# The first tile of a two-layer MLP begun by halves of 256 tokens, with attention of the second half between

## The chip, the cores and the metric

The kernel runs on one core of one Trainium2 chip. The metric is device time in microseconds (us). Engines are TensorE (PE, with its weight loads shown apart as PEld), VectorE (DVE), ScalarE (ACT), GpSimd (POOL) and SyncE (SP); SP, ACT and POOL issue DMAs, and 16 DMA engines carry them. Each engine works through its instructions in the order in which they were written.

## The reference

Local attention with 8 memory rows, then two MLPs whose hidden activations differ.

```python
for c in range(nc):                                   # chunks of 32 queries
    l_start, r_end = max(0, c*32 - 16), min(S, c*32 + 32 + 8)
    k_full = concat([mem_k, k[:, :, l_start:r_end]], axis=2)
    v_full = concat([mem_v, v[:, :, l_start:r_end]], axis=2)
    scores = scale * (q_c @ k_full.T)
    a = exp(scores - max(scores)); a = a / (sum(a) + 1e-9)
    out[:, :, chunk] = a @ v_full
x = out as (3072 tokens, 512)
h = x @ w_in;   g = maximum(0.01 * h, h);   y = g @ w_out          # 512 -> 2048 -> 512
h = y @ w_in2;  g = P(h) / (Q(h) + 1e-6);   out = g @ w_out2       # P, Q polynomials
```

There are 4 batches, 8 heads of 64, 768 positions. w_in, w_out and the second layer's weights come as 64-bit floats.

## The kernel before

The 3072 tokens are cut into 6 tiles of 512 (NMAX), a tile into 4 blocks of 128. Attention works on blocks, numbered j from 0. The hidden width of 2048 is cut into 16 pairs f: the 128 columns of w_in and the 128 rows of w_out that belong together. One pair on one tile is an h (`emit_h`, 12 matmuls into a bank "hps": 4 steps over 512 inputs, 3 products each) and a y (`emit_y`, 12 matmuls into the four banks "acc", which gather over all pairs). Each fp32 number is carried as a high and a low part: xh and xl for the activations, wih/wil and woh/wol for the weights, gh and gl for the hidden values, and the three products are high x high, high x low and low x high. Between h and y, ACT makes gh and s (`leaky`), and DVE makes gl from them.

Weights arrive as raw 64-bit words (tile "wr", three buffers, 512 KB a load) and pass four steps: `load_w` issues the DMA on SP, `scale_w` is an ACT instruction (ww from wr), `join_w` three DVE instructions (ww), `split_w` an ACT cast (wih or woh) and a DVE subtraction (wil or wol). `weights0` does one of each for the first layer: cast of one half-pair, scaling of the one two further on, join of the next, subtraction, and a further load. The list `halves` sets the order of the half-pairs, "i" for w_in and "o" for w_out.

Attention of a block is a row of functions: `mid_load_q`, `mid_load_k`, `mid_load_v` issue its DMAs; `mid_a` transposes q and k on PE (psq, psk) and copies them on ACT (qT, pb); `mid_s` makes the scores on PE (pss) and on DVE their maxima and differences (mx, t); `mid_e` is the exponential on ACT; `mid_n` the division on DVE (sm, t); `mid_p` transposes the weights on PE (pst) with a copy on ACT (pm); `mid_x` the weighted sums on PE (psx), then xh by ACT and xl by DVE. Blocks 0 to 3, the whole first tile, come in a prologue that is written out line by line; blocks 4 to 7 go between the matmuls of the first tile, and later ones are made by another route between those of later tiles.

Nothing reorders: the written order is each engine's order. After the prologue a loop goes over `items`, one for each layer, tile and pair; `advance_h` runs h two items ahead of y, and in the first tile calls `weights0` for each h from the third on, while another `weights0` follows each y. k and v of blocks 0, 1 and 2 stand in three different buffers (`room`): kb and vb, and the still unused tiles xh and xl of the second token tile.

Of the kernel before, what the change touches and what calls it, by code (L numbers as in the profile page):

```python
# [9 lines left out]
F32 = mybir.dt.float32  # L10
# [6 lines left out]
P = 128  # L17
LCTX, RCTX, CHUNK = 16, 8, 32
NEG = -1.0e30
WIDE_FROM = 2  # L20


@with_exitstack
def kernel(
# [76 lines left out]

    halves = []
    for layer in range(2):
        for f in range(FC + 2):
            if f < FC:
                halves.append((layer, "i", f))
            if f >= 2:
                halves.append((layer, "o", f - 2))

# [116 lines left out]
    LAST = WIDE_FROM * FIRST  # L226
    spare = [xpool.tile([P, 2, 2 * H * D], F32R, tag=t, name=t).bitcast(F32) for t in ("xh", "xl")]
    room = [(kw, vflat), (spare[0][:, 0], spare[0][:, 1]), (spare[1][:, 0], spare[1][:, 1])]
    mem_in = {}
    mq, mqT, mm = {}, {}, {}  # L230

    def home(j):
        return j if j < len(room) else 0

# [16 lines left out]
    def mid_load_k(j):  # L251
        bi, blk = divmod(j, WPS)
        t = room[home(j)][0].rearrange("p (n h d) -> p n h d", n=2, h=H)
        eng = nc.gpsimd if j else nc.sync
        if mem_rows("k", j, bi):
            for n in range(2):
                for row in (0, NM + CTX):
                    eng.dma_start(out=t[row:row + NM, n], in_=mem_k[bi].rearrange("h p d -> p h d"))
# [368 lines left out]
    def emit_y(c):  # L627
        layer, i, f = items[c]
        s0, n = tiles_of[layer][i]
        if f == 0:  # L630
            acc[i] = [psa.tile([P, 512], F32, tag="acc", name="acc") for _ in range(KC)]
        gh, gl = gt.pop(c)
        wh, wl = wt[0, "o", f]
        for d in range(KC):
            ws = slice(d * P, (d + 1) * P)
            for m, (w_, g_) in enumerate(((wh, gh), (wh, gl), (wl, gh))):
                nc.tensor.matmul(acc[i][d][:, :n], w_[:, ws], g_,  # L637
                                 start=(f == 0 and m == 0), stop=(f == FC - 1 and m == 2))
        if f == FC - 1:
# [46 lines left out]
    with tc.manual_schedule():  # L686
        nc.scalar.preload_act_table_set("natural_log_exp_and_others")
        make_identity(nc, ident)
        nc.vector.memset(kb[0][0:32], 0.0)
        for hh in range(2):  # L690
            nc.vector.memset(vw[hh * WIN:hh * WIN + 32, 0], 0.0)
        nc.vector.memset(lnb, ONE * 2.0 ** -LN_SHIFT)
        nc.vector.memset(expb, -LN_SHIFT * math.log(2.0))
        mid_load_q(0)
        mid_load_k(0)
        mid_load_v(0)
        load_w(FC * 2)
        for j in (1, 2):
            mid_load_q(j)
            mid_load_k(j)  # L700
            mid_load_v(j)
            if j == 1:
                load_w(FC * 2)
        mid_load_q(3)
        mid_a(0)
        mid_load_k(3)
        mid_s(0)
        mid_e(0)
        scale_w(FC * 2)
        mid_a(1)  # L710
        mid_n(0)
        mid_s(1)
        mid_p(0)
        mid_e(1)
        mid_x(0)
        mid_load_v(3)
        load_w(FC * 2)
        join_w(FC * 2)
        scale_w(FC * 2)
        mid_a(2)  # L720
        mid_n(1)
        mid_s(2)
        mid_p(1)
        mid_e(2)
        mid_x(1)
        load_w(FC * 2)
        weights0()
        mid_a(3)
        mid_n(2)
        mid_load_q(FIRST)  # L730
        mid_load_k(FIRST)
        mid_s(3)
        mid_p(2)
        mid_e(3)
        mid_x(2)
        weights0()
        mid_n(3)
        mid_p(3)
        mid_x(3)
        mid_load_v(FIRST)  # L740
        weights0()
        weights0()
        nc.sync.dma_start(out=coef[:, 0:4], in_=a.partition_broadcast(P))
        nc.sync.dma_start(out=coef[:, 4:6], in_=b.partition_broadcast(P))
# [21 lines left out]
        advance_h(LA)
        weights0()
        for c in range(len(items)):
            layer, i, f = items[c]
# [77 lines left out]
```

## Time and profile before

| | before |
|---|---|
| median of 3 runs | 1170.08 us (1169.69 to 1170.71) |
| profiled execution, its own time | 1169.41 us |
| its span | 1167.6 us |
| PE busy | 1131.2 us, 97% |
| weight loads (PEld) | 928.6 us, 80% |
| DVE busy | 771.6 us, 66% |
| ACT busy | 624.9 us, 54% |
| POOL busy | 247.5 us, 21% |
| mean granted clock of PE | 0.989 |

The span runs from the first instruction to the last; about 2 us of the execution lie outside it. A share of busy time is a mean over stages: the first 57 us, without wide matmuls, are hardly seen in PE's 97%. A row of the timeline gives start and length in us, engine and line, what was written from what, the shape, the count, and in brackets the idle time before it and what ended it.

### The profile page before, as it was taken

Reading aid. Unit: us, or ns where it says so; the run is one execution under the profiler, and the core shown is the slowest. Engines: PE = TensorE matmul, PEld = TensorE weight load, DVE = VectorE, ACT = ScalarE, POOL = GpSimd, SP = SyncE. Lnnn points to the kernel's source line nnn. Section 1 sums busy time; section 2 is a strip of 40 time slices with the busy share of each in tenths; the row PEclk is TensorE's granted clock in tenths of the full one; section 3 lists DMA queues with packets and bytes.
Section 4 is the critical chain, followed back from the end, with each engine's and each line's share of the span. In section 5 each row is a group of like instructions: output and inputs, shape, how many; then the busy total and the mean of one; then the engine's idle time right before and its main releaser. Section 6 shows DMA issues by size and latency. Waiting matters only on the chain.

```text
span 1167.6 us, 20228 instructions
## 1 busy us (share of the span) xinstructions
PE 1131.2 (97%) x7808; PEld 928.6 (80%) x7808; DVE 771.6 (66%) x1361; ACT 624.9 (54%) x1135; POOL 247.5 (21%) x298
## 2 busy tenths in 40 slices
PE   5599999999999999999999999999999999999998
PEld 3487778888888888888888888888888888888887
DVE  3478865555546554554234888788788788788775
ACT  3367643223223223222344877777777777777765
POOL 6000131233211231111000222222222222222222
PEclk9699999999999999999999999999999999999999
DMA  8556788788878677852343200200200200200000
GB/s 161 136 162 197 196 226 231 198 219 243 212 202 228 197 214 223 228 170 70 131 131 91 90 1 1 72 1 1 72 1 1 73 1 1 73 1 1 37 1 36
DMA packets 149005, 132.18 MB, mean 113 GB/s; under 512 B 63473, under 2 KB 119377, under 8 KB 148909
## 3 DMA queue, kind: packets, MB, share of 16 engines
q1 hardware_dynamic: 140869, 122.54, 36.5%
q0 software_dynamic: 6272, 7.92, 3.1%
q8 instruction: 62, 1.02, 0.4%
q10 hardware_dynamic: 1768, 0.43, 0.2%
q14 instruction: 34, 0.28, 0.1%
HBM read 93.06 MB, written 37.75 MB: 112 GB/s over the span
## 4 chain that ended last, share of the span: by engine, by line
PE 91%; DMA 3%; ACT 2%; DVE 2%; issue 1%; SPq 1%; ACTq 0%; DVEq 0%
PE hps L579 44%; PE acc L675 22%; PE acc L637 20%; PE psx L379 2%; DMA wr<-in_moe_w_in_dram 1%; PE pss L475 1%; ACT t L343 1%; DMA xl<-in_k_dram 1%; DVE ww L149 1%; DMA xh<-in_v_dram 0%; DMA vb<-in_v_dram 0%; SPq L262 0%; ACT ww L132 0%; DVE wol L167 0%; PE pst L364 0%
## 5 line engine op out<-in xcount | busy, mean ns | idle before, releaser
L615 POOL TENSOR_TENSOR gl<-R,gh 128x512 fp32r<-128x512 f32 x96 | 125.7, 1309 | 502.1 <-ACT gh L614 459.9
L589 ACT ACTIVATE gh<-hps 128x512 fp32r<-128x512 f32 x96 | 57.5, 599 | 291.6 <-PE hps L579 291.6
L592 DVE TENSOR_TENSOR gl<-s,gh 128x512 fp32r<-128x512 f32 x96 | 66.3, 691 | 191.6 <-ACT s L590 188.4
L579 PE MATMUL hps<-xh,wih 128*128 128x512 f32 x384 | 154.0, 401 | 2.3 <-ACT pm L365 1.9
L637 PE MATMUL acc<-gh,woh 128*128 128x512 f32 x384 | 150.8, 393 | 0.0
L579 PE MATMUL hps<-xl,wih 128*128 128x512 f32 x384 | 150.8, 393 | 0.0
L579 PE MATMUL hps<-xh,wil 128*128 128x512 f32 x384 | 150.7, 392 | 0.0
L637 PE MATMUL acc<-gl,woh 128*128 128x512 f32 x384 | 149.6, 389 | 0.0
L637 PE MATMUL acc<-gh,wol 128*128 128x512 f32 x384 | 149.5, 389 | 0.0
L579 PE MATMUL hps<-yh,wih 128*128 128x512 f32 x384 | 149.4, 389 | 0.0
L579 PE MATMUL hps<-yl,wih 128*128 128x512 f32 x384 | 149.4, 389 | 0.0
L579 PE MATMUL hps<-yh,wil 128*128 128x512 f32 x384 | 149.4, 389 | 0.0
L675 PE MATMUL acc<-woh,gh 128*128 128x512 f32 x384 | 149.4, 389 | 0.0
L675 PE MATMUL acc<-wol,gh 128*128 128x512 f32 x384 | 149.4, 389 | 0.0
L675 PE MATMUL acc<-woh,gl 128*128 128x512 f32 x384 | 149.4, 389 | 0.0
L440 POOL DMA_DIRECT2D vb<-in_v_dram x128 | 83.4, 653 | 252.4 <-PE psx L379 199.6
L602 ACT ACTIVATE A<-hps 128x512 f32<-128x512 f32 x96 | 57.1, 595 | 114.0 <-PE hps L579 114.0
L618 DVE SCALAR_TENSOR_TENSOR A<-A,small,pb 128x512 f32<-128x512 f32 x96 | 72.0, 750 | 56.5 <-ACT pb L603 56.5
L579 PEld LDWEIGHTS hps<-xh,wih 128*128 128x128 f32 x384 | 72.7, 189 | 18.8 <-ACT pm L365 2.3
L609 DVE SCALAR_TENSOR_TENSOR A<-A,pb 128x512 f32<-128x512 f32 x96 | 66.5, 692 | 30.0 <-ACT pb L622 30.0
L579 PEld LDWEIGHTS hps<-xh,wil 128*128 128x128 f32 x384 | 72.8, 190 | 15.4
L579 PEld LDWEIGHTS hps<-xl,wih 128*128 128x128 f32 x384 | 72.8, 190 | 14.6 <-DVE xl L388 0.2
(107 smaller groups left out, 2017.4 us busy)
## 6 DMA issues: line engine op xcount, KB each, us to landing
wr<-in_moe_w_in_dram SPq DMA_DIRECT2D x32, 512.0 KB
wr<-in_moe_w_out_dram SPq DMA_DIRECT2D x32, 512.0 KB
park_dram<-pb SPq DMA_DIRECT2D x16, 512.0 KB
pb<-park_dram SPq DMA_DIRECT2D x64, 128.0 KB
w_dram<-ww SPq DMA_DIRECT2D x32, 256.0 KB
wb<-w_dram SPq DMA_DIRECT2D x32, 256.0 KB
kb<-in_k_dram SPq DMA_DIRECT2D x59, 112.0 KB
vb<-in_v_dram POOLq DMA_DIRECT2D x118, 56.0 KB, 3.5
```

Of the source, the lines that this page charges most:

```text
L149: nc.vector.scalar_tensor_tensor(out=wu, in0=lo32, scalar=29, in1=wu, op0=ALU.logical_shift_right, op1=ALU.bitwise_or)
L379: nc.tensor.matmul(ps[hh][e * 64:e * 64 + 64, i, c * CHUNK:(c + 1) * CHUNK], vt[r, c, 2 * i + e, :], weight(r, c, i, e), start=True, stop= ...
L440: nc.gpsimd.dma_start(out=vw[r + at:r + at + n, c], in_=v[bi, hs, lo:lo + n, :].rearrange("h p d -> p h d"))
L579: nc.tensor.matmul(ps[:, :n], w_[:, ws], x_[:, kk, :], start=(kk == 0 and m == 0), stop=(kk == KC - 1 and m == 2))
L589: nc.scalar.activation(out=gh, in_=ps, func=AF.Prelu, alpha=0.01)
L592: return [lambda: nc.vector.tensor_tensor(out=gl, in0=s, in1=gh.bitcast(F32), op=ALU.subtract)]
L602: nc.scalar.activation(out=A, in_=ps, func=AF.Square)
L609: nc.vector.scalar_tensor_tensor(out=A0, in0=A0, scalar=ONE, in1=U0, op0=ALU.add, op1=ALU.mult)
L615: nc.gpsimd.tensor_tensor(out=gl, in0=R0, in1=gh.bitcast(F32), op=ALU.subtract)
L618: nc.vector.scalar_tensor_tensor(out=A, in0=A, scalar=babs[:, 1:2], in1=U, op0=ALU.mult, op1=ALU.add)
L637: nc.tensor.matmul(acc[i][d][:, :n], w_[:, ws], g_, start=(f == 0 and m == 0), stop=(f == FC - 1 and m == 2))
L675: nc.tensor.matmul(acc[i][s], g_[:, ss], w_, start=(f == 0 and m == 0), stop=(f == FC - 1 and m == 2))
```

## The change

The 512 tokens of the first tile are taken in two halves of 256 for the first four pairs (AHEAD). The prologue does attention of blocks 0 and 1, then h and y of pairs 0 to 3 on 256 tokens, and puts blocks 2 and 3 between them. Then the same four pairs follow on the other 256 tokens, and pairs 4 to 15 on all 512. `halves` is reordered, so that the weights of pairs 0 to 3 come first. The scores and weighted sums of blocks 2 and 3 now use the PSUM banks "ps" that h uses, since "acc" is taken. k and v of blocks 0 to 3 share two buffers in turn. The memory rows of k of block 0 are issued on POOL and no longer on SP, q and k of block 0 ahead of the identity matrix.

```diff
+AHEAD = 4
...
+    HALF = NMAX // 2
+    halves = [(0, "i", 0), (0, "i", 1), (0, "i", 2), (0, "o", 0), (0, "i", 3), (0, "o", 1)]
+    for f in range(2, AHEAD):
+        halves.append((0, "o", f))
+    for f in range(AHEAD, FC + 2):
+        if f < FC:
+            halves.append((0, "i", f))
+        if f >= AHEAD + 2:
+            halves.append((0, "o", f - 2))
...
     def home(j):
-        return j if j < len(room) else 0
+        return j % 2 if j < FIRST else 0
...
     def mid_bank(j, name):
-        if j < FIRST:
+        if j < HALF // P:
             return psa.tile([P, 512], F32, tag="acc", name=name)
...
+    items = [(0, 0, f, lo, HALF) for lo in (0, HALF) for f in range(AHEAD)]
+    items += [(l, i, f, 0, tiles_of[l][i][1]) for l in range(2) for i in range(len(tiles_of[l])) for f in range(FC)
+              if (l, i) != (0, 0) or f >= AHEAD]
...
-                nc.tensor.matmul(ps[:, :n], w_[:, ws], x_[:, kk, :],
+                nc.tensor.matmul(ps[:, :n], w_[:, ws], x_[:, kk, lo:lo + n],
...
+        mid_a(0)
+        mid_load_q(2)
+        mid_load_k(2)
+        mid_s(0)
+        mid_e(0)
+        mid_a(1)
+        scale_w(FC * 2)
+        mid_n(0)
+        mid_load_q(3)
+        mid_load_k(3)
+        join_w(FC * 2)
+        mid_s(1)
+        mid_p(0)
+        mid_e(1)
+        mid_n(1)
+        mid_x(0)
+        mid_load_v(2)
+        scale_w(FC * 2)
+        weights0()
+        mid_p(1)
+        mid_x(1)
+        mid_load_v(3)
+        weights0()
+        advance_h(2)
+        weights0()
+        weights0()
+        advance_h(3)
+        emit_y(0)
+        mid_a(2)
+        mid_s(2)
+        mid_e(2)
+        weights0()
+        advance_h(4)
+        mid_n(2)
+        weights0()
+        emit_y(1)
+        mid_p(2)
+        mid_a(3)
...
+        mid_x(2)
+        mid_s(3)
+        mid_e(3)
+        weights0()
+        emit_y(2)
+        mid_n(3)
+        weights0()
+        mid_p(3)
+        emit_y(3)
+        mid_x(3)
```

What this does to the engines' order is seen at three places. On ACT, at the end of block 1's weighted sum (xh from psx; block 3's before): what stands ahead of the first hidden values gh and s, and between them. ww from wr is the scaling of newly landed weights. Before:

```order
L365 COPY pm<-pst 128x512
L387 CAST xh<-psx 128x2x128 x2
L164 CAST wih<-ww 128x512
L132 ACTIVATE ww<-wr 128x512
L164 CAST woh<-ww 128x512
L132 ACTIVATE ww<-wr 128x512
L589 ACTIVATE gh<-hps 128x512
L590 ACTIVATE s<-hps 128x512
```

Now:

```order
L373 COPY pm<-pst 128x512
L395 CAST xh<-psx 128x2x128 x2
L173 CAST wih<-ww 128x512
L141 ACTIVATE ww<-wr 128x512
L597 ACTIVATE gh<-hps 128x256
L598 ACTIVATE s<-hps 128x256
L597 ACTIVATE gh<-hps 128x256
L598 ACTIVATE s<-hps 128x256
L173 CAST wih<-ww 128x512
L141 ACTIVATE ww<-wr 128x512
```

The first gh stands two blocks earlier and behind the scaling of the fourth half-pair (it was the sixth before).

On PE, where the first matmuls of layer 1 stand, behind the weighted sum of a block (psx). Before, behind block 3:

```order
L320 MATMUL pss<-pb,qT 32x64 x32
L364 MATMUL pst<-ident,t 128x128 x4
L379 MATMUL psx<-pm,xl 64x32 x32
L364 MATMUL pst<-ident,t 128x128 x4
L379 MATMUL psx<-pm,vb 64x32 x32
L579 MATMUL hps<-xh,wih 128x512
L579 MATMUL hps<-xl,wih 128x512
L579 MATMUL hps<-xh,wil 128x512
```

Now, the middle of the first half: the end of y of pair 1, block 2's p, block 3's a, block 2's x, block 3's s, and the start of y of pair 2:

```order
L645 MATMUL acc<-gl,woh 128x256
L645 MATMUL acc<-gh,wol 128x256
L372 MATMUL pst<-ident,t 128x128 x4
L305 MATMUL psq<-ident,q_244 128x128 x4
L314 MATMUL psk<-ident,xh 128x104 x8
L387 MATMUL psx<-pm,vb 64x32 x32
L328 MATMUL pss<-pb,qT 32x64 x32
L645 MATMUL acc<-gh,woh 128x256
L645 MATMUL acc<-gl,woh 128x256
L645 MATMUL acc<-gh,wol 128x256
```

Attention of blocks 2 and 3, which stood ahead of every wide matmul, stands between the narrow ones.

On DVE, the same stretch. Before, the end of the prologue: block 2's low part, one half-pair joined and split, block 3's division and low part.

```order
L388 TENSOR_TENSOR xl<-psx,xh 128x2x128 x2
L146 TENSOR_SCALAR ww<-ww 128x512
L149 SCALAR_TENSOR_TENSOR ww<-wr,ww 128x512
L153 SCALAR_TENSOR_TENSOR ww<-wr,ww 128x512
L167 TENSOR_TENSOR wil<-ww,wih 128x512
L352 TENSOR_REDUCE sm<-t 128x8
L355 TENSOR_SCALAR sm<-sm 128x8
L356 RECIPROCAL sm<-sm 128x8
L357 TENSOR_TENSOR t<-t,sm 128x512
L388 TENSOR_TENSOR xl<-psx,xh 128x2x128 x2
```

Now, from the low part of pair 3's input weights on: gl of pair 3, block 2's division, a half-pair joined and split, block 2's low part, and the first of block 3's maxima.

```order
L176 TENSOR_TENSOR wil<-ww,wih 128x512
L600 TENSOR_TENSOR gl<-s,gh 128x256
L360 TENSOR_REDUCE sm<-t 128x8
L363 TENSOR_SCALAR sm<-sm 128x8
L364 RECIPROCAL sm<-sm 128x8
L365 TENSOR_TENSOR t<-t,sm 128x512
L155 TENSOR_SCALAR ww<-ww 128x512
L158 SCALAR_TENSOR_TENSOR ww<-wr,ww 128x512
L162 SCALAR_TENSOR_TENSOR ww<-wr,ww 128x512
L176 TENSOR_TENSOR wol<-ww,woh 128x512
L396 TENSOR_TENSOR xl<-psx,xh 128x2x128 x2
L337 TENSOR_REDUCE mx<-pss 128x4
```

A block's division stands behind a gl, which needs an h, which needs the low part of its weights; before, there was no gl in the prologue.

## Rows read from the trace of the kernel before

**Rows 1.** Waits of PE from 57 us on: total, times, longest

```profile
PE pst L364 <- DVE t L357: 2.8, 1, 2.8
PE hps L579 <- ACT pm L365: 1.9, 2, 1.0
```

**Rows 2.** Stretches: PE, PEld, DVE, ACT, POOL busy; clock; DMA share; GB/s

```profile
0.00:20.00 20.00, 8.86 (x153) 6.18 (x153) 4.77 (x15) 5.46 (x9) 15.55 (x33) 1.00 0.82 153
20.00:32.00 12.00, 8.82 (x162) 6.79 (x162) 7.33 (x17) 5.02 (x10) 2.76 (x6) 1.00 0.88 182
32.00:36.00 4.00, 4.00 (x74) 3.74 (x70) 1.89 (x5) 1.31 (x4) 0.00 (x0) 1.00 0.48 91
36.00:40.00 4.00, 0.04 (x1) 0.00 (x0) 2.84 (x6) 0.00 (x0) 0.00 (x0) 0.91 0.79 228
40.00:44.00 4.00, 1.93 (x66) 1.54 (x67) 0.40 (x1) 1.95 (x4) 0.00 (x0) 0.50 1.08 300
44.00:57.00 13.00, 5.89 (x136) 4.85 (x134) 5.93 (x14) 3.76 (x9) 0.00 (x0) 0.50 0.24 61
```

**Rows 3.** Timeline of PE in the prologue, and the first wide matmuls

```profile
27.09 0.93 PE L306 MATMUL psk<-ident,xl 104*128 104x104 f32 x4 [0.93 <-DMA xl<-in_k_dram]
...
31.66 2.03 PE L379 MATMUL psx<-pm,xh 64*64 64x32 f32 x64 [0.73 <-ACT pm L365]
33.62 1.11 PE L297 MATMUL psq<-ident,q 128*128 128x128 f32 x4
34.53 1.51 PE L306 MATMUL psk<-ident,kb 104*128 104x104 f32 x8
42.07 1.62 PE L320 MATMUL pss<-pb,qT 64*32 64x64 f32 x64 [6.02 <-ACT pb L307]
...
57.10 0.80 PE L579 MATMUL hps<-xh,wih 128*128 128x512 f32 x1 [0.36 <-ACT xh L387]
...
59.00 0.63 PE L579 MATMUL hps<-xl,wih 128*128 128x512 f32 x1
59.43 0.63 PE L579 MATMUL hps<-xh,wil 128*128 128x512 f32 x1
```

**Rows 4.** Timeline of PE behind the rise of its clock

```profile
63.22 0.39 PE L579 MATMUL hps<-xh,wil 128*128 128x512 f32 x1
...
70.98 0.60 PE L297 MATMUL psq<-ident,qr 128*128 128x128 f32 x4
```

**Rows 5.** The chain, one group of 12 wide matmuls: start, length

```profile
157.84 2.72 PE hps L579 x12
```

**Rows 6.** Timeline of ACT in the prologue

```profile
31.51 0.63 ACT L338 ACTIVATE t<-t 128x512 f32<-128x512 f32 x1
33.63 0.65 ACT L387 CAST xh<-psx 128x256 fp32r<-128x256 f32 x2 [1.49 <-PE psx L379]
...
40.47 0.66 ACT L132 ACTIVATE ww<-wr 128x512 f32<-128x512 f32 x1 [5.67 <-DMA wr<-in_moe_w_in_dram]
```

**Rows 7.** Timeline of SP's queue: the memory rows of block 0

```profile
1.42 4.21 SPq L258 DMA_DIRECT2D kb<-in_mem_k_dram  x4
```

**Rows 8.** The page's costliest groups: a weight load's row

```profile
L579 PEld LDWEIGHTS hps<-xh,wih 128*128 128x128 f32 x384 | 72.7, 189 | 18.8 <-ACT pm L365 2.3
```

**Rows 9.** Timeline of DVE in the prologue

```profile
29.79 0.42 DVE L329 TENSOR_REDUCE mx<-pss 128x4 f32<-128x256 f32 x1 [1.34 <-PE pss L320]
...
34.04 0.76 DVE L388 TENSOR_TENSOR xl<-psx,xh 128x256 fp32r<-128x256 f32 x2 [2.58 <-ACT xh L387]
34.71 0.42 DVE L146 TENSOR_SCALAR ww<-ww 128x512 uint32<-128x512 uint32 x1
...
37.10 0.68 DVE L352 TENSOR_REDUCE sm<-t 128x8 f32<-128x512 f32 x1
...
38.26 0.69 DVE L357 TENSOR_TENSOR t<-t,sm 128x512 f32<-128x512 f32 x1
```

More of the change, by code (lines that the diff above doesn't have):

```diff
@@ L95 @@
     ONE = 1.0 + 1e-6
[L102 to L108, printed above, removed]
+    HALF = NMAX // 2
[7 more added lines that the diff above has]
+            halves.append((0, "o", f - 2))
+    for f in range(FC + 2):
+        if f < FC:
+            halves.append((1, "i", f))
+        if f >= 2:
+            halves.append((1, "o", f - 2))
+    assert len(set(halves)) == len(halves) == 4 * FC
     wt, wraw, wsum = {}, {}, {}
@@ L257, in mid_load_k @@
                 for row in (0, NM + CTX):
-                    eng.dma_start(out=t[row:row + NM, n], in_=mem_k[bi].rearrange("h p d -> p h d"))
+                    nc.gpsimd.dma_start(out=t[row:row + NM, n], in_=mem_k[bi].rearrange("h p d -> p h d"))
         for n in range(2):
@@ L627, in emit_y @@
     def emit_y(c):
-        layer, i, f = items[c]
-        s0, n = tiles_of[layer][i]
-        if f == 0:
+        layer, i, f, lo, n = items[c]
+        s0 = tiles_of[layer][i][0]
+        if f == 0 and lo == 0:
             acc[i] = [psa.tile([P, 512], F32, tag="acc", name="acc") for _ in range(KC)]
@@ L636, in emit_y @@
             for m, (w_, g_) in enumerate(((wh, gh), (wh, gl), (wl, gh))):
-                nc.tensor.matmul(acc[i][d][:, :n], w_[:, ws], g_,
-                                 start=(f == 0 and m == 0), stop=(f == FC - 1 and m == 2))
+                nc.tensor.matmul(acc[i][d][:, lo:lo + n], w_[:, ws], g_,
+                                 start=(f == 0 and lo == 0 and m == 0), stop=(f == FC - 1 and m == 2))
         if f == FC - 1:
@@ L691 @@
             nc.vector.memset(vw[hh * WIN:hh * WIN + 32, 0], 0.0)
+        mid_load_q(0)
+        mid_load_k(0)
+        make_identity(nc, ident)
         nc.vector.memset(lnb, ONE * 2.0 ** -LN_SHIFT)
         nc.vector.memset(expb, -LN_SHIFT * math.log(2.0))
-        mid_load_q(0)
-        mid_load_k(0)
         mid_load_v(0)
+        mid_load_q(1)
+        mid_load_k(1)
         load_w(FC * 2)
[L698 to L716, printed above, removed]
-        load_w(FC * 2)
[L718 to L725, printed above, removed]
-        load_w(FC * 2)
[L727 to L744, printed above, removed]
+        mid_load_v(1)
+        load_w(FC * 2)
+        load_w(FC * 2)
         issued_h = [0]
@@ L751, in advance_h @@
                 emit_h(c)
-                if c < NA:
+                if items[c][0] == 0:
                     steps = leaky(c)
-                    if LA <= c < FC:
+                    if AHEAD <= c and items[c][1] == 0:
                         weights0(steps)
@@ L763, in advance_h @@
                     rational(c + 1, False, True)
+        mid_a(0)
[36 more added lines that the diff above has]
+        mid_a(3)
+        mid_load_q(FIRST)
+        mid_load_k(FIRST)
+        mid_x(2)
[8 more added lines that the diff above has]
+        mid_x(3)
+        mid_load_v(FIRST)
+        nc.sync.dma_start(out=coef[:, 0:4], in_=a.partition_broadcast(P))
+        nc.sync.dma_start(out=coef[:, 4:6], in_=b.partition_broadcast(P))
         plan()
[L766 to L769, printed above, removed]
+        advance_h(AHEAD + LA)
+        for c in range(AHEAD, len(items)):
+            layer, i, f = items[c][:3]
+            g = c - AHEAD
             if layer == 0:
-                if c == FC:
+                if g == FC:
                     nc.scalar.mul(out=ncf, in_=coef[:, 0:4], mul=-1.0)
@@ L804 @@
                 advance_h(c + 1 + look)
-            wide(2 * c + 1)
+            wide(2 * g + 1)
             if i == 0 and layer == 0:
-                weights0()
+                if f >= AHEAD:
+                    weights0()
                 if n_split[0] == FC * 2 and n_load[0] < FC * 2 + 2:
```

27 lines of the change are left out of this document (11 added, 16 removed).

## The prediction

> **What bounds the kernel now.** I read the waits of TensorE (PE) first. From 57 us to the end PE waits 2.8 us for one VectorE (DVE) instruction and 1.9 us for ScalarE (ACT) [rows 1]: from the first wide matmul on, PE is the bound, and the end moves only with the moment at which that stream begins and with what is in it. So I read next what comes before it. The stretches [rows 2] show a prologue limited by transfers and by chains across engines: the DMA engines are busy 0.82 to 0.88 of the time to 32 us, PE works 0.04 us between 36 and 40 and 5.9 of the 13 us from 44 to 57. The timeline of PE [rows 3] has the first wide matmul at 57.10 us. Those 57 us are what the change can win from.
>
> PE's speed in that prologue is the second thing to see. The granted clock reads 1.00 until 36 and 0.50 from 40 to 57 [rows 2], but four transposes of 128 columns take 1.11 us at 33.62 [rows 3] and 0.60 at 70.98 [rows 4], so I price the prologue at the lower level (1.2 GHz) from its start. The 512-column matmuls stand 0.43 us apart there (59.00 to 59.43) and 2.72/12 = 0.227 later [rows 3, 5]. The clock rose near 63.2, after PE had worked without a pause since 57.10 [rows 3, 4].
>
> **What is moved.** I call T the moment from which PE runs without stops: 57.1 before, the start of the second half's first matmul after. The stream behind T loses the first halves of four pairs: 8 groups of 12 matmuls, 96 x 0.227/2 = 10.9 us at the upper level. The same 96 stand before T instead, with two blocks of attention between them. Everything hangs on what T becomes. The change is a gain while T stays under 57.1 + 10.9 plus small terms, about 69 us.
>
> **T, first part: to the end of y of pair 0.** Before T eight halves of weights must now be cast, joined and split, not two. I count them W0 to W8 in their new order: in 0, in 1, in 2, out 0, in 3, out 1, out 2, out 3, in 4.
> - ACT stands in order, and scaling W3 now stands ahead of gh of the first two groups. In the old order ACT sat 5.67 us behind such a scaling whose weights had not landed [rows 6].
> - When W3 lands: ahead of it on the queues are q and k of four blocks, v of three (128x8x64 and 56x4x64 floats: some 3.8 MB), 0.25 MB of memory rows, and W0 to W3 of 0.52 MB each: 6.1 MB. The stretches give 20 x 153 GB/s = 3.06 MB by 20 us, 5.24 by 32, 5.61 by 36, 6.52 by 40 [rows 2], so 38 us at the old pace. Without the slack at 32 to 36 (DMA share 0.48), and with the share of wide packets that gave 300 GB/s at 40 to 44, some 32. I take 35. The four k rows of memory that leave SP's queue (4.21 us of issuing [rows 7]) start block 0 about 4 us earlier; on POOL they stand ahead of the memory rows of block 1, which so gains little.
> - The weighted sum of block 1 ended at 33.69 [rows 3]; with block 2 no longer ahead of it I take 29 to 31. Two groups behind it end at 34.5 to 36.5, about when W3 is scaled, so an earlier W3 alone would win little.
> - A 256-column matmul does not occur in the trace. At the lower level it lies between 0.23 (a 128-column transpose, 33.62 to 34.53 for four) and 0.43 (512 columns) [rows 3]; at the upper, by the same ratio of levels, between 0.12 and 0.227. I take the lower ends, since the columns alone make half of 0.43 and of 0.227. Second half at 0.12 instead of 0.113: 96 x 0.007 = +0.6 us. If the weight load showed through (0.189 each [rows 8]): 96 x 0.076 = +7.3, the upper bound.
> - From W3: scale 0.65, gh and s of two groups 4 x 0.33 [rows 6], gl 0.38, join and split together 2.39 [rows 9]: the low part of in 2 at 39.7. Its group waits for it at its third matmul; ten are left, 2.3 us: 42.0. y of pair 0: 12 x 0.23, to 44.8.
>
> The Trainium skill, "TensorE: Matmul & The Clock Gate", section on LDWEIGHTS, says that a load's time goes by its columns alone; 128 columns at 1.2 GHz are by that an estimated 107 ns. By that price the second half's loads lie just under its 0.113 of streaming and cost nothing. The row, 0.189, speaks against that and gives the upper bound; no row here has 256 columns.
>
> **T, second part: 44.8 us to the second half.** PE, ACT and DVE each keep the written order, so this is one chain. PE's order is a2, s2, h3, y1, p2, a3, x2, s3, y2, p3, y3, x3 (a transposes, s scores, p transposes of weights, x weighted sums); each group of 12 waits at its third matmul for the low part that DVE subtracts.
> 1. a2 and s2 to the first reduction: transposes 0.91 + 0.75, then 27.09 to 29.79 = 2.70 [rows 3, 9]: 4.36. DVE to the exponential: 29.79 to 31.51 = 1.72 [rows 6, 9].
> 2. join W5 and split W4, 34.71 to 37.10 = 2.39; rest of h3 2.30; gh, s, gl 0.65 + 0.38; n2 1.85 (37.10 to 38.95), which stands behind gl on DVE; join W6, split W5 2.39 [rows 6, 9]; rest of y1 2.30. To here 18.3.
> 3. p2 0.91, a3 2.42, x2 2.03, s3 1.62 on PE [rows 3]: 7.0. DVE has only x2's low part meanwhile.
> 4. scores 1.72, join and split 2.39, n3 1.85, join and split 2.39: 8.35 of DVE, over which y2 and p3 are hidden. Rest of y3 2.30, x3 2.03, cast 0.4: 13.1.
> Together 38.4, so T = 83.2. DVE's own work in it is about 19 us: half of the stretch DVE waits for PE, and half PE for DVE.
>
> **The sum.** T +26.1; moved work -10.9; narrow matmuls +0.6. The slow start of the stream, 14 matmuls in 6.12 us (57.10 to 63.22) instead of 3.2, which cost 2.9 us, is mostly over by T, as y3 and x3 run up to it without a pause: -1.9 (between 0 and -2.9). PE's waits after T: behind it DVE has per pair 2 x 2.39 and a gl, about 5.5 us, against 5.44 of PE plus attention, as before, and the lead in halves is the same by the code; I leave the 4.7 us where they are (bounds: all gone, or as much again). Sum +13.9 on the profiled execution's 1169.41 (span 1167.6): 1183.3. The median shown is 0.7 above that execution, less than a measurement can tell; I give 1183.
>
> **A rule weighed.** Between 44 and 57 us PE worked 5.9 of 13 us, with waits between, and stayed at the lower level (granted 0.50 [rows 2]). The new stretch is of that kind: matmuls for 2.3 us, then 1 to 4 us of waiting. The Trainium skill, "TensorE: Matmul & The Clock Gate", section "HAM oscillation — how this bites in real kernels", has bursts that are shorter than the waits between them fall back to the lower clock each time. The trace agrees; by that rule the time is my 1183, without it the first rival's.
>
> **The rivals.**
> - The clock rises early. PE has more to do than before (some 24 of 38 us), and h0 and h1 run without a pause. At the upper level PE's parts halve: 1.5 in a2 and s2, 3.3 in the rests of three groups, 3.5 in step 3, 1.0 in x3, 2.4 in the first part: 11.7 less, T = 71.5, +14.4 - 10.9 - 2.9 + 0.6 = +1.2: 1170.6. Against it: at 20 to 32 us PE was busy 8.8 of 12 us [rows 2] and its rows stayed long.
> - Faster: the clock rises, and W3 to W7 also land 5 us earlier, as they would if the queue held the 300 GB/s of 40 to 44 us [rows 2] from 25 us on; ACT then never stands. T = 66.5, +9.4 - 10.9 - 2.9 + 0.6 = -3.8: 1165.6. It decides at T = 69. Against it: the small packets of v lie between the weights, and the two groups behind block 1 bound it at 34.5.
> - Slower still: the weight load shows through in the second half: 1183.3 + 7.3 = 1191.
> - The change does not do what it says: if nothing of the first half overlapped the attention of the second, T would be 57.1 plus 8 x 12 x 0.23 = 22.1, so 79.2, and the time 1169.4 + 22.1 - 10.9 - 1.9 + 0.6 = 1179.3. It lies inside my range; PE's waits would tell it from the chain.
>
> **How the numbers follow.** The chain at the lower level, with W3 at 32 to 38 and single terms 2 us off, the last rival within it: 0.64, 1176 to 1189. Clock up for part or all: 0.16, 1169 to 1176. Faster rival 0.10. Slower still 0.10. The range 1170 to 1190 leaves out the faster rival, a little of the second case and half of the last. A measurement here tells 0.2% (2.3 us) from no change: faster, under 1167.7, 0.11 (the faster rival and 0.01 of the second case); within, 0.09 of the second case; slower 0.80.
>
> **What would show it.** In the new trace: ACT waits for W3 ahead of gh with PE idle around 35 us; PE waits for wil and wol before the third matmul of h2, h3, y1, y3; DVE waits for PE while p2, a3, x2, s3 run; 256-column matmuls 0.21 to 0.23 apart before T and 0.11 to 0.12 behind; T at 80 to 85. I am wrong if T lies under 70, if the first half's rows show 0.12 spacing, or if PE waits over 9 us behind T.

## The result, and the profile after

The changed kernel takes 1177.95 us (median of 4 runs, 1177.03 to 1180.84) against 1170.39 us for the kernel before beside it (4 runs, 1169.69 to 1171.24): ratio 1.0068, 95% interval 1.0050 to 1.0087. It is slower, by 7.6 us; 1183 was predicted, some 13 us slower, within 1170 to 1190. The profiled execution of the changed kernel is its slowest, 1180.84 us with a span of 1179.1.

T, the moment from which TensorE (PE) runs without stops, is 80.38 us, against 57.10 before [rows 3]; 80 to 85 was expected. The timeline of PE, changed kernel: the end of block 1's sum, four places in the first half, the start of the second half.

```profile
29.01 2.30 PE L387 MATMUL psx<-pm,xh 64*64 64x32 f32 x64 [0.73 <-ACT pm L373]
31.65 0.58 PE L587 MATMUL hps<-xh,wih 128*128 128x256 f32 x1 [0.34 <-ACT xh L395]
...
32.70 0.41 PE L587 MATMUL hps<-xh,wih 128*128 128x256 f32 x1
32.92 0.41 PE L587 MATMUL hps<-xl,wih 128*128 128x256 f32 x1
...
35.35 0.28 PE L587 MATMUL hps<-xl,wih 128*128 128x256 f32 x1
35.47 0.28 PE L587 MATMUL hps<-xh,wil 128*128 128x256 f32 x1
...
40.05 0.58 PE L587 MATMUL hps<-xh,wil 128*128 128x256 f32 x1 [1.84 <-DVE wil L176]
...
62.29 0.58 PE L645 MATMUL acc<-gh,wol 128*128 128x256 f32 x1 [3.31 <-DVE wol L176]
...
66.91 1.16 PE L387 MATMUL psx<-pm,vb 64*64 64x32 f32 x64
68.00 0.86 PE L328 MATMUL pss<-pb,qT 64*32 64x64 f32 x64
72.04 0.39 PE L645 MATMUL acc<-gh,woh 128*128 128x256 f32 x1 [3.18 <-ACT woh L173]
...
80.38 0.38 PE L587 MATMUL hps<-xh,wih 128*128 128x256 f32 x1 [0.46 <-ACT xh L395]
...
81.17 0.28 PE L587 MATMUL hps<-xh,wih 128*128 128x256 f32 x1
81.30 0.28 PE L587 MATMUL hps<-xl,wih 128*128 128x256 f32 x1
```

Narrow matmuls stand 0.22 us apart at 32.70 and 0.12 at 35.35 and behind 80.38: both prices of the prediction, so the clock rose once already at 35. PE's waits in the changed kernel (us, times, longest), first from 0 to 80 us (the rows on the first half), then from 80 us to the end:

```profile
PE acc L645 <- DVE wol L176: 6.0, 4, 3.3
...
PE acc L645 <- ACT woh L173: 4.4, 2, 3.2
PE hps L587 <- ACT wih L173: 4.2, 2, 2.9
...
PE hps L587 <- DVE wil L176: 2.2, 2, 1.8
```

```profile
PE pst L372 <- DVE t L365: 2.8, 1, 2.8
PE pss L328 <- ACT pb L315: 1.2, 1, 1.2
PE hps L587 <- ACT xh L395: 0.5, 1, 0.5
PE hps L587 <- ACT pm L373: 0.4, 1, 0.4
```

Before T PE waits 16.8 us for cast and low parts of weights; behind T they are 4.4 us (the wait of 0.5 ends at T itself), against 4.7 before [rows 1]. That those weights are late has a reason on the other two engines. Timeline of ScalarE (ACT), then of VectorE (DVE), changed kernel:

```profile
35.05 0.68 ACT L141 ACTIVATE ww<-wr 128x512 f32<-128x512 f32 x1 [2.66 <-DMA wr<-in_moe_w_out_dram]
35.63 0.37 ACT L597 ACTIVATE gh<-hps 128x256 fp32r<-128x256 f32 x1
...
40.93 0.69 ACT L141 ACTIVATE ww<-wr 128x512 f32<-128x512 f32 x1 [3.27 <-DMA wr<-in_moe_w_in_dram]
```

```profile
50.32 0.42 DVE L337 TENSOR_REDUCE mx<-pss 128x4 f32<-128x256 f32 x1 [5.85 <-PE pss L328]
...
57.66 0.42 DVE L600 TENSOR_TENSOR gl<-s,gh 128x256 fp32r<-128x256 f32 x1 [3.28 <-ACT s L598]
...
68.48 0.76 DVE L396 TENSOR_TENSOR xl<-psx,xh 128x256 fp32r<-128x256 f32 x2 [6.25 <-ACT xh L395]
```

ACT stands for W3 and W4 to land. DVE stands 5.85 us until a2 and s2 are done, 3.28 for h3 and 6.25 through p2, a3 and x2, and in each such gap no join or split was written that it could have done. The stretches of the changed kernel (columns as in [rows 2]):

```profile
44.00:57.00 13.00, 9.10 (x98) 7.94 (x98) 4.38 (x10) 3.36 (x7) 0.00 (x0) 0.63 0.27 81
57.00:70.00 13.00, 7.36 (x156) 6.74 (x156) 5.89 (x14) 4.34 (x10) 0.00 (x0) 0.66 0.40 91
70.00:80.00 10.00, 6.43 (x92) 5.78 (x92) 7.08 (x15) 3.54 (x7) 0.00 (x0) 0.83 0.42 101
80.00:100.00 20.00, 18.26 (x184) 16.67 (x185) 14.44 (x29) 13.39 (x41) 0.00 (x0) 1.00 0.61 163
160.00:200.00 40.00, 39.47 (x347) 32.04 (x348) 21.66 (x49) 14.17 (x28) 9.76 (x16) 0.96 0.73 212
```

From 44 to 80 PE is busy 22.9 of 36 us and DVE 17.4: neither is full, each waits for the other. The granted clock is a mixture there, 0.63 to 0.83, and not the 0.50 that I had taken.

For the profiled executions: T +23.3; moved work -10.9; slow start gone, -2.9; narrow matmuls of the second half +0.5 (0.119 against 0.1135 us, half of a wide one's 0.227; 96 of them); waits -0.3. That is +9.7, and the span grew by 11.5. Of the rest, 1.8, the clock explains 1.6: it fell once more (0.96 from 160 to 200 us), and eight wide matmuls from 161.46 to 164.86 us stand 0.43 us apart instead of 0.227.

### The profile page after: what moved, and what is told of

Its sections match the earlier page's. It is cut to its first block, busy times and chain, and to the rows that moved or that the text cites. A ratio compares the mean times of both kernels' runs of the same rounds, so it can differ in the third digit from the quotient of the medians.

```text
span 1179.1 us, 20405 instructions
## 1 busy us (share of the span) xinstructions
PE 1136.9 (96%) x7904; PEld 937.9 (80%) x7904; DVE 772.1 (65%) x1365; ACT 625.6 (53%) x1143; POOL 242.7 (21%) x290
## 4 chain that ended last, share of the span: by engine, by line
PE 89%; DMA 4%; DVE 4%; ACT 1%; issue 1%; SPq 1%; ACTq 0%
PE hps L587 43%; PE acc L683 22%; PE acc L645 20%; PE psx L387 2%; DMA wr<-in_moe_w_in_dram 2%; PE pss L483 1%; DMA vb<-in_v_dram 1%; DVE ww L158 1%; DVE ww L162 1%; DVE ww L155 0%; DMA xh<-in_k_dram 0%; DMA xh<-in_v_dram 0%; DVE wol L176 0%; ACT t L351 0%; SPq L293 0%
## 5 line engine op out<-in xcount | busy, mean ns | idle before, releaser
L597 ACT ACTIVATE gh<-hps 128x512 fp32r<-128x512 f32 (+1 forms) x100 | 58.2, 582 | 298.3 <-PE hps L587 298.3
L600 DVE TENSOR_TENSOR gl<-s,gh 128x512 fp32r<-128x512 f32 (+1 forms) x100 | 67.0, 670 | 199.2 <-ACT s L598 196.3
L587 PE MATMUL hps<-xh,wih 128*128 128x512 f32 (+1 forms) x400 | 158.2, 396 | 5.4 <-ACT wih L173 4.2
L645 PE MATMUL acc<-gh,wol 128*128 128x512 f32 (+1 forms) x400 | 154.5, 386 | 6.0 <-DVE wol L176 6.0
L645 PE MATMUL acc<-gh,woh 128*128 128x512 f32 (+1 forms) x400 | 155.5, 389 | 4.4 <-ACT woh L173 4.4
L587 PE MATMUL hps<-xh,wil 128*128 128x512 f32 (+1 forms) x400 | 155.2, 388 | 2.2 <-DVE wil L176 2.2
L587 PE MATMUL hps<-xl,wih 128*128 128x512 f32 (+1 forms) x400 | 154.9, 387 | 0.1
L645 PE MATMUL acc<-gl,woh 128*128 128x512 f32 (+1 forms) x400 | 153.8, 384 | 0.0
L645 PEld LDWEIGHTS acc<-gh,wol 128*128 128x128 f32 x400 | 76.7, 192 | 21.5 <-DVE wol L176 7.0
L645 PEld LDWEIGHTS acc<-gh,woh 128*128 128x128 f32 x400 | 76.6, 192 | 19.8 <-ACT woh L173 4.9
L587 PEld LDWEIGHTS hps<-xh,wil 128*128 128x128 f32 x400 | 77.2, 193 | 17.4 <-DVE wil L176 2.7
```

The lines of the kernel that those rows point to most:

```text
L587: nc.tensor.matmul(ps[:, :n], w_[:, ws], x_[:, kk, lo:lo + n], start=(kk == 0 and m == 0), stop=(kk == KC - 1 and m == 2))
L597: nc.scalar.activation(out=gh, in_=ps, func=AF.Prelu, alpha=0.01)
L600: return [lambda: nc.vector.tensor_tensor(out=gl, in0=s, in1=gh.bitcast(F32), op=ALU.subtract)]
L645: nc.tensor.matmul(acc[i][d][:, lo:lo + n], w_[:, ws], g_, start=(f == 0 and lo == 0 and m == 0), stop=(f == FC - 1 and m == 2))
```

## The experiments

All kernels in one table. T and span come from the profiled execution; "stream" is span less T, all that follows T. The kernel before beside each group of runs had a median of 1168.4 to 1168.9 us (15, 13, 17 and 11 runs).

| kernel | pairs by halves | T | stream | median us | ratio to before, 95% |
|---|---|---|---|---|---|
| before | 0 | 57.10 | 1110.5 | 1170.39 | |
| changed | 4 | 80.38 | 1098.7 | 1177.95 | 1.0050 to 1.0087 |
| e1 the same again | 4 | 77.90 | 1096.6 | 1178.91 | 1.0071 to 1.0101 |
| e2 v late | 4 | 77.55 | 1099.0 | 1178.26 | 1.0071 to 1.0096 |
| e3 weights early | 4 | 71.88 | 1098.1 | 1173.82 | 1.0029 to 1.0057 |
| e4 old start | 4 | 80.60 | 1098.6 | 1179.51 | 1.0075 to 1.0105 |
| e5 both gates | 4 | 76.59 | 1098.4 | 1174.63 | 1.0043 to 1.0068 |
| e6 gates and order | 4 | 70.68 | 1097.9 | 1171.35 | 1.0016 to 1.0036 |
| e7 two pairs | 2 | 61.91 | 1112.9 | 1176.96 | 1.0056 to 1.0081 |
| e8 two pairs, lead | 2 | 55.85 | 1106.5 | 1163.09 | 0.9939 to 0.9965 |
| e9 scores first | 2 | 52.49 | 1106.5 | 1160.66 | 0.9912 to 0.9950 |
| e10 three pairs | 3 | 59.77 | 1102.2 | 1160.72 | 0.9919 to 0.9959 |
| e11 no halves | 0 | 49.38 | 1110.9 | 1162.06 | 0.9930 to 0.9962 |
| e12 four pairs | 4 | 70.58 | 1101.9 | 1173.47 | 1.0027 to 1.0054 |

**e1**, the changed kernel again, beside e2 to e4.

> The changed kernel once more, nothing edited, to see how far its times and its stretches differ from execution to execution. The theory of the in-order chain (T, the start of the second half's first matmul, is set by ACT standing for the fourth half-pair of weights and then by PE, ACT and DVE waiting for each other) has T at 80 us within 1.5, and +7 to +11 us against before. The rival, that what differs is behind T (clock, or PE's waits at 90 to 200 us), has T the same in both executions and the difference of up to 3.8 us behind it.

Its executions reach from 1176.25 to 1181.62, and T was 77.90 in the profiled one. So T itself differs by 2.5 us from one execution to the next: here y0 waited for nothing, ran at the upper level of the clock from its fourth matmul on and ended at 44.48; in the profile above it waited 1.20 us for wol, ran at the lower level and ended at 46.48. Against the kernel before beside it, the same program is 10.4 us slower here, where the first measurement had 7.6. e2 to e4 are best held against e1, which ran beside them.

**e2**, v of blocks 2 and 3 loaded behind the weights.

```diff
         mid_x(0)
-        mid_load_v(2)
...
-        mid_load_v(3)
...
         weights0()
+        mid_load_v(2)
+        mid_load_v(3)
         advance_h(3)
```

> The loads of v of blocks 2 and 3 are issued behind the fourth call of weights0, so the DMAs of W3 to W6 no longer stand behind them. Chain theory: ACT stood 2.7 us for W3 (scaled at 35.05) and 3.3 us for W4 (40.9); both go, block 1's two groups (end at 36.2) bound instead, the end of y of pair 0 moves from 46.5 to about 43.5 and T from 80.4 to about 77.5: 3 us less than the changed kernel. Rival A, that transfers are hidden anyway and only the chain behind y of pair 0 counts: within 1 us of it. Rival B, that v of blocks 2 and 3 then comes late: x2 or x3 waits, 1 to 4 us more.

Nothing was won. The timeline of ACT in e2, the scaling of W3 and the first gh:

```profile
31.65 0.72 ACT L141 ACTIVATE ww<-wr 128x512 f32<-128x512 f32 x1
...
34.23 0.38 ACT L597 ACTIVATE gh<-hps 128x256 fp32r<-128x256 f32 x1 [1.87 <-PE hps L587]
```

W3 is scaled 3.4 us earlier than in the changed kernel's profile and without a wait, but then ACT stands for PE: block 1's sum ends at 30.7 (31.3 there), and the second group ends where it did.

**e4**, the other side alone: identity matrix first and block 0's memory rows on SP, as before the change, so that block 1 is early.

```diff
+        make_identity(nc, ident)
...
-        mid_load_q(0)
-        mid_load_k(0)
-        make_identity(nc, ident)
...
+        mid_load_q(0)
+        mid_load_k(0)
...
-                    nc.gpsimd.dma_start(out=t[row:row + NM, n], in_=mem_k[bi]...
+                    (nc.gpsimd if j else nc.sync).dma_start(out=t[row:row + NM, n], in_=mem_k[bi]...
```

> The first instructions as before the change: identity first on POOL, block 0's memory rows of k on SP ahead of its k, q and k behind the constants. All else as changed. Chain theory: the start of block 0 (psq at 4.8 us, k of block 1 at 17.7) is hidden behind the landing of W3, which the bytes ahead of it set: within 1.5 us of the changed kernel. Rival, that the new start itself costs (PE waits 4.8 us for the identity, k of block 1 lands 2 us later than before): 2 to 3 us less than the changed kernel.

Nothing either. The first narrow matmul starts at 28.1, 3.6 us sooner, and now ACT stands for W3, the timeline of ACT in e4:

```profile
37.05 0.66 ACT L141 ACTIVATE ww<-wr 128x512 f32<-128x512 f32 x1 [8.24 <-DMA wr<-in_moe_w_out_dram]
```

**e5**, e2 and e4 together.

> Both edits that changed nothing by themselves, together: v of blocks 2 and 3 loaded behind W3 to W6, and the first instructions as before the change. In the one, W3 was early and PE waited for block 1 (its weighted sum ended at 30.7); in the other, block 1 was early (27.8) and ACT stood 5.6 us until W3. Theory of two gates side by side, each hiding the other: together they move the first wait of the third group, and all behind it, by 2.5 to 3.5 us; T near 74.5, the time 3 us under the changed kernel. Rival, that both arrive late for one reason (the DMA engines are full until 32 us, so what one gains the other loses): within 1 us of the changed kernel.

1174.63: 3.6 us under e2, 4.9 under e4. Two gates stood side by side, each hidden by the other; opening one alone gave nothing, both gave 4 by the medians. The profile shows less of it at T: the third group starts at 35.38, 2.8 us sooner than in e1 (38.14), as the theory had it, but T is 76.59, only 1.3 sooner and not the 74.5 expected. That execution was the slowest of the five; in it PE ran the whole of y0 at the lower level.

**e3**, the order of DVE's weights alone: a `weights0` right behind y0 (DVE's gap to 50.32), and two ahead of x2 (its gap to 68.48).

```diff
         emit_y(0)
+        weights0()
         mid_a(2)
...
         mid_n(2)
-        weights0()
         emit_y(1)
...
+        weights0()
+        weights0()
         mid_x(2)
...
-        weights0()
         emit_y(2)
         mid_n(3)
-        weights0()
         mid_p(3)
```

> The order of the second part of the first half: the calls of weights0 stand earlier, so that DVE joins weights while PE does attention (one ahead of block 2's transposes, one ahead of h of pair 3, two ahead of block 2's weighted sum). Nothing else differs. Chain theory: DVE's idle times of 5.9, 3.3 and 6.3 us (at 44, 54 and 62 us) are filled, PE's waits for wil and wol of pairs 1 to 3 (0.4 + 3.3 + 0.7 + 0.7 us) and for the casts (2.9 + 1.3 + 3.2 us) mostly go; T from 80.4 to about 75: 5 to 6 us less than the changed kernel. Rival, that PE at its lower clock is the bound of that stretch: within 1 us of the changed kernel.

T fell by 6 us against e1, the median by 5.1; the times scatter (1169.66 to 1177.00, 11 runs), but the intervals of e3 and e1 do not overlap. PE's waits for weights went from 15.4 us in e1 to 5.1. The same instructions, moved into gaps that the trace showed, are worth that much; so the chain of mutual waits is shown, not only argued. The longest wait left in e3 is PE's for block 3's division:

```profile
66.86 1.09 PE L372 MATMUL pst<-ident,t 128*128 128x128 f32 x4 [5.82 <-DVE t L365]
...
71.88 0.38 PE L587 MATMUL hps<-xh,wih 128*128 128x256 f32 x1 [0.46 <-ACT xh L395]
```

**e6**, e2, e3 and e4 together.

> The same with the calls of weights0 earlier as well (which alone gave 5 us). Chain theory: the gains add, T from 77.9 by 6 and by 3 to near 69, which is the break-even of the prediction: the time within 2 us of before. Rival, that DVE, full from 43 to 66 us when weights are joined early, is then the bound of its own: T stays at 71 to 72 and the time 3 to 5 us over before.

T 70.68 and 1171.35: the change repaired at each place found so far is still slower than before, by 0.16 to 0.36%. T lies between the theory's 69 and the rival's 71 to 72. The rival had DVE down as full from 43 to 66 us; that row of the stretches of e6 speaks against it: DVE is busy 14.67 of 23 us, PE 15.37, at a clock of 0.70.

```profile
43.00:66.00 23.00, 15.37 (x247) 13.66 (x248) 14.67 (x31) 8.62 (x18) 0.00 (x0) 0.70 0.64 159
```

**e7**, two pairs only, with e4's start.

```diff
-AHEAD = 4
+AHEAD = 2
...
         advance_h(2)
-        weights0()
-        weights0()
-        advance_h(3)
-        emit_y(0)
         mid_a(2)
         mid_s(2)
         mid_e(2)
         weights0()
-        advance_h(4)
         mid_n(2)
-        weights0()
-        emit_y(1)
+        emit_y(0)
```

(y1 goes where y2 stood; y2, y3 and the last `weights0` are gone; the half-pairs come as in 0, in 1, out 0, out 1, then in pairs as before.)

> Two pairs are begun by halves, not four (AHEAD = 2): h of pairs 0 and 1 behind block 1, y of pair 0 behind block 2's scores, y of pair 1 behind block 3's; the first instructions as before the change. Theory that the price is VectorE's: each pair begun early needs 4.8 us of DVE for its two half-pairs ahead of T and takes 2.7 us of PE from behind it, so pairs pay only as long as DVE has idle time (some 10 us at 39 to 57 before the change, two pairs' worth): T stays at 56 to 60, 5.4 us less work behind it, and the time is 2 to 6 us under before. Rival, that attention between narrow matmuls is what costs, however many pairs (PE waits, the lower clock): T at 63 or more, the time 0 to 3 us over before.

The gain did not come: T is 61.91, and the time 8.4 us over before, more than the rival allowed. W3's load stands behind v of block 2 on SP's queue, and ACT stood for it; and behind T, where the work of two pairs left 5.4 us, PE waits for weights. ACT's timeline, and PE's waits from T on:

```profile
36.36 0.66 ACT L139 ACTIVATE ww<-wr 128x512 f32<-128x512 f32 x1 [7.31 <-DMA wr<-in_moe_w_out_dram]
```

```profile
PE hps L585 <- DVE wil L174: 3.5, 4, 1.4
PE acc L643 <- DVE wol L174: 2.4, 4, 1.1
...
PE acc L643 <- ACT woh L171: 1.5, 3, 0.6
```

Its stream, 1112.9, is longer than the kernel's before, though it holds less work. Weights must not only be in time at T; they must be ahead.

**e8**, e7 with W3 loaded at once behind the first join, v behind weights, and one more half-pair prepared before T.

```diff
         mid_n(0)
+        join_w(FC * 2)
+        load_w(FC * 2)
         mid_load_q(3)
         mid_load_k(3)
-        join_w(FC * 2)
...
-        mid_load_v(2)
         scale_w(FC * 2)
         weights0()
+        mid_load_v(2)
...
         mid_a(2)
+        weights0()
         mid_s(2)
         mid_e(2)
-        weights0()
         mid_n(2)
         emit_y(0)
+        weights0()
         mid_p(2)
```

> Two pairs by halves as in e7, but the fourth half-pair is loaded right behind the first join, ahead of q and k of block 3 and of v of blocks 2 and 3, and one more weights0 stands in VectorE's idle time behind block 2's transposes. Theory (what the halves cost is late weights, before T as at ScalarE's 7.3 us and behind T as 8.6 us of TensorE's waits): ScalarE's wait goes, T falls from 61.9 to 57-59, the waits behind T fall to 4-6 us, so against the kernel before T +1, moved work -5.4, slow start -2, narrow matmuls +0.3: 5 to 7 us faster than it, 0.994 to 0.996. Rival (VectorE has no room for it, the lead stays short): T 59-62 and over 7 us of waits behind it, within 2 us of the kernel before.

As the theory had it: T 55.85, a microsecond earlier than it said, and 5.8 us faster than before. None of PE's waits behind T is for weights any more; the two long ones are for attention, as in the kernel before [rows 1]:

```profile
PE pst L370 <- DVE t L363: 2.8, 1, 2.8
PE hps L585 <- ACT pm L371: 1.9, 2, 1.0
```

**e9**, e8 with block 3's transposes and scores ahead of block 2's p and x.

```diff
         emit_y(0)
-        weights0()
-        mid_p(2)
         mid_a(3)
...
-        mid_x(2)
         mid_s(3)
         mid_e(3)
-        mid_n(3)
+        mid_p(2)
         weights0()
+        mid_x(2)
+        mid_n(3)
         emit_y(1)
+        weights0()
         mid_p(3)
```

> e8 with block 3's transposes and scores ahead of block 2's transposed weights and weighted sum, so that TensorE does something while VectorE divides. Theory (before T the three engines wait for one another in turn, and another written order fills that): T 52-55, 9 to 11 us faster than the kernel before. Rival (ScalarE's and VectorE's own work is the bound there already): T within 1 us of e8's, and the time within 2 us of it.

T 52.49, as the theory had it, and 8.2 us faster than before (9 to 11 expected): 2.4 under e8 in the medians, with intervals that overlap a little. That lies 0.4 us outside the rival's 2 us, and T fell by 3.4 where the rival allowed 1.

**e10**, e9 with a third pair (half-pairs in the order in 0, in 1, out 0, in 2, out 1, out 2).

```diff
-AHEAD = 2
+AHEAD = 3
...
         mid_n(2)
+        weights0()
         emit_y(0)
...
         mid_e(3)
+        advance_h(3)
         mid_p(2)
...
         mid_p(3)
+        emit_y(2)
         mid_x(3)
```

> e9 with three pairs by halves: one more first half, 2.7 us taken from behind T, for two more half-pairs that VectorE must join and split before T (4.8 us). Theory of e6 (VectorE is full before T, a pair costs more than it takes): T 4 to 6 us later than e9's, the time 1 to 3 us above e9's. Rival (VectorE still has 6 to 8 us of idle time there): T 1 to 2 us later, the time 1 to 2 us below e9's.

T rose by 7.3 and the stream fell by 4.3, so 3.0 us lost in the profiled executions; the medians are the same (1160.72 and 1160.66). Neither gain nor, with certainty, loss. Neither theory nor rival has the reason right. The stretch from 44 to 57 us, e9's row and then e10's:

```profile
44.00:57.00 13.00, 11.25 (x166) 10.38 (x167) 8.04 (x18) 5.77 (x14) 0.00 (x0) 0.65 0.52 134
...
44.00:57.00 13.00, 11.42 (x105) 10.36 (x106) 8.83 (x19) 5.29 (x11) 0.00 (x0) 0.51 0.66 181
```

DVE is not full in e10, 8.83 of 13 us, and PE waits little: it is busy for 11.42 us, but at the lower level nearly throughout (0.51). The third pair's h takes 3.2 us there and its y 3.9, 7.1 together with waits of 0.67 and 0.85 in them, where its 24 matmuls at 0.12 would take 2.9. So T rose by PE's own work at the lower clock more than by waits.

**e11**, e9's order without any halves.

```diff
-AHEAD = 2
+AHEAD = 0
...
-        advance_h(2)
         mid_a(2)
-        weights0()
         mid_s(2)
...
-        emit_y(0)
...
-        emit_y(1)
-        weights0()
         mid_p(3)
```

> No halves at all: every pair on all 512 tokens, as in the kernel before, but with e9's order of loads and of attention in the prologue. Theory (the halves themselves pay when they stand in TensorE's idle time): T 51-54, 3 to 5 us faster than the kernel before, and 4 to 6 us slower than e9. Rival (only the order of the prologue pays): the time within 2 us of e9's.

The rival holds: 1162.06 is within 2 us of e9, and 6.8 us faster than before, of the 8.2 that e9 won. That is won by the order of loads and of attention together; e11 also keeps the changed kernel's buffers for k, v and scores, and no run separates these. The largest reason that the traces show stands in the kernel before: ACT stood 5.67 us at 40.47 for weights to land [rows 6], ahead of block 3's qT and pb, and PE 6.02 us at 42.07 for that pb [rows 3]. In e11 the loads are early: the same scaling (W2) waits 0.41 us at 24.36, and the next one, which now stands ahead of block 2's qT, not at all. Timelines of ACT and of PE in e11, PE's with block 3's scores and T:

```profile
24.36 0.68 ACT L139 ACTIVATE ww<-wr 128x512 f32<-128x512 f32 x1 [0.41 <-DMA wr<-in_moe_w_in_dram]
...
29.34 0.68 ACT L139 ACTIVATE ww<-wr 128x512 f32<-128x512 f32 x1
29.92 0.58 ACT L305 ACTIVATE qT<-psq 128x512 f32<-128x512 f32 x1
```

```profile
35.74 1.56 PE L326 MATMUL pss<-pb,qT 64*32 64x64 f32 x64 [0.81 <-ACT pb L313]
...
49.38 0.80 PE L585 MATMUL hps<-xh,wih 128*128 128x512 f32 x1 [0.36 <-ACT xh L393]
```

**e12**, four pairs in e10's order (half-pairs in 0, in 1, out 0, in 2, out 1, in 3, out 2, out 3).

```diff
-AHEAD = 3
+AHEAD = 4
...
         mid_p(3)
+        advance_h(4)
+        weights0()
         emit_y(2)
         mid_x(3)
+        weights0()
+        emit_y(3)
```

> The change itself, four pairs by halves, in the order of e10: weights split just ahead of their use, block 3's transposes and scores ahead of block 2's weighted sum, the last hidden group and two y behind block 3's transposed weights. Theory (each further pair lengthens the chain before T by about what it takes from behind it, so the number of pairs hardly matters and the order does): T 64-67 against 80, moved work -10.9, slow start -2.9, narrow +0.5: 3 to 8 us faster than the kernel before, 0.993 to 0.9975. Rival (four pairs cannot be fed before T, VectorE's eight joins and splits set it, as supposed in e6): T 69-72 as in e6, within 2 us of the kernel before or above it.

My theory fell: T 70.58, as in e6, and 0.4% slower than before. The rival has T right, but its reason is not shown: DVE is busy 24.43 of 38 us from 28 to 66. The last two y wait again for weights, and PE runs them at the lower level; the timeline of PE and the stretches of e12:

```profile
60.27 0.58 PE L643 MATMUL acc<-gh,wol 128*128 128x256 f32 x1 [1.55 <-DVE wol L174]
60.66 0.41 PE L643 MATMUL acc<-gh,woh 128*128 128x256 f32 x1
60.87 0.41 PE L643 MATMUL acc<-gl,woh 128*128 128x256 f32 x1
...
68.28 0.58 PE L643 MATMUL acc<-gh,wol 128*128 128x256 f32 x1 [1.59 <-DVE wol L174]
```

```profile
28.00:66.00 38.00, 28.01 (x375) 24.34 (x373) 24.43 (x51) 16.93 (x38) 0.00 (x0) 0.80 0.62 152
...
80.00:100.00 20.00, 18.63 (x280) 16.48 (x280) 12.01 (x25) 13.64 (x40) 2.40 (x4) 0.91 0.53 143
```

Read down the table in one order of work, e11, e9, e10, e12: T is 49.4, 52.5, 59.8 and 70.6, the stream 1110.9, 1106.5, 1102.2 and 1101.9. The first two pairs cost T 3.1 us together and take 4.4 from the stream; the third costs 7.3 and takes 4.3; the fourth costs 10.8 and takes 0.3 (e6, with the same T, has a stream of 1097.9, so about 4 could be had; in e12 the clock fell again at 80 to 100 us, 0.91). The first two stand in part where PE waits anyway: its wait for block 3's division, 3.01 us at 45.17 in e11, is 0.15 at 49.45 in e9. The third adds mostly PE's own work at the lower level. With the fourth the mutual waits come back: from 41 us to T PE waits 3.6 us in e9, 4.3 in e10 and 10.2 in e12. Each of these profiles is of one execution, and e1 showed that T can differ by 2.5 us between two.

## Why the prediction was right

The kernel is slower, and for the reason given: T moves by more than the stream gives back. The size was too high: about 13 us were forecast, and the medians lie 7.6 us apart here and 10.4 in e1. Step by step:

- **First part of T.** Block 1's sum was to end at 29 to 31: it ended at 31.3. W3 was to be scaled at 35: 35.05, with ACT waiting ahead of gh. The low part of in 2 was to be there at 39.7: the matmul that waits for it starts at 40.05. Right to half a microsecond. "An earlier W3 alone would win little" is e2: 0.65 us by the medians, less than the intervals. The end of y0 was set at 44.8 and came at 46.48 (44.48 in e1): the scaling of W4 also stood for its load, 3.27 us (1.15 in e1), which I had not counted.
- **Second part, mis-sized.** 38.4 us predicted from y0's end to the second half; 33.9 in the profile (80.38 less 46.48), 33.4 in e1 (77.90 less 44.48). The chain was the one described: waits for wil, wih, woh and wol on PE, DVE standing through p2, a3 and x2. The clock was the error: x2 took 1.16 us, s3 0.86 and x3 1.14, where I had 2.03, 1.62 and 2.03; a3 took 1.5 and the rest of y3 1.4, where I had 2.42 and 2.30. These five are 4.4 of the 4.5 us.
- **A rule weighed.** By the rows the clock was up at 35.35, low at 40.05 and 62.29, up again from 66.91 to 72.04, and low after the wait of 0.71 us that ended at 73.26. The Trainium skill, "TensorE: Matmul & The Clock Gate", section "HAM oscillation — how this bites in real kernels", has bursts that are shorter than the waits around them fall back, and the trace agrees: the rows low at 40.05 and 73.26 follow bursts of two matmuls, 0.5 us, between waits of 1.25 and 1.84 us and of 3.18 and 0.71. As a price for the whole stretch it was too strict, since longer unbroken work of PE did raise the clock here: from 62.29 to 68.86 PE never waited, and x2 and s3 at its end ran at the upper level. The first rival thus came true for a part of the stretch.
- **Slow start, mis-sized.** -1.9 was taken, between 0 and -2.9: the second half runs at 0.12 us a matmul from its third on, so nearly all 2.9 came back.
- **Narrow matmuls.** +0.6 forecast, +0.5 measured. The rival in which weight loads show through, +7.3, is refuted: 0.12 apart with a new weight at each matmul.
- **Waits behind T.** 4.7 forecast as unchanged, 4.4 measured.
- **Does not do what it says.** T lies near that rival's 79.2, but by another way: in 44 to 80 us PE's rows alternate between both kinds of work with waits for weights, and e3's moving of weights alone cut T by 6, which it could not if the two merely stood one behind the other.

The forecast for the profiled execution was 1183.3. The second part takes 4.5 from it, the slow start 1.0, the narrow matmuls 0.1 and the waits 0.3; y0's delay adds 1.7 and the fall of the clock behind 160 us 1.6, which makes 1180.7 against 1180.84 measured. That it lies as near as that is partly luck: the two additions were not foreseen, and e1, the same program, has neither. There the same working gives 1183.3 - 5.0 - 1.0 - 0.1 - 0.6 (waits behind T 4.1) - 0.3 (y0) = 1176.3 against 1176.25.

What stays open: whether the halves pay anything over e11. e9's 1160.66 and e11's 1162.06 cannot be told apart by six runs each. Open too is how much of e11's gain is the order of loads and how much that of attention, and why the clock stayed low so long in e10.

## What to carry over

A wait that hides another gives nothing when it is removed alone; look at what stands next to it in time and open both. Before work is brought forward into a prologue, ask which in-order engine must prepare its operands and whether its gaps are where these are needed: here the first two pairs together took 4.4 us from behind T and put 3.1 in front of it, while the third put 7.3 and the fourth 10.8. Ask also at which clock the moved work will run. And read the waits of the kernel before once more: an ACT instruction waited 5.67 us for a load, with the next block's copies queued behind it. An order of the prologue in which that wait is gone gained 6.8 us, where the change lost 7.6.

## What the hardware showed that I had not expected

- The clock rose within PE's first unbroken stretch of narrow matmuls (0.21 us apart up to 35.05, 0.12 from 35.23 on), and was low again in the row behind waits of 1.25 and 1.84 us (40.05).
- In e10 it stayed low through work that was nearly as unbroken: busy 11.42 of 13 us from 44 to 57 with no wait over 0.85, PE still ran narrow matmuls 0.21 us apart, and went on so until 64.66.
- Behind a 2.80 us wait for a block's division, which ended at 160.53, the clock fell once in the changed kernel (0.96 over 160 to 200 us) and not in e1, which is the same program and has the same wait (2.83 us; 1.00).
- The granted clock that is recorded for the first 36 us does not tell the level: 20 to 32 us reads 1.00 in e8 and 0.50 in e9 and e11, and block 1's four transposes take 1.09 us in all three.
